# Row layout of a DRAM buffer, splits moved from GpSimd to VectorE, and token tasks of the third stage moved under the last slots of the second

## The chip, the cores and the metric

The kernel runs on one core of one Trainium2 chip. The time is the device time of one execution in microseconds; that of the kernel before is the median of three runs. Names of engines: PE is TensorE (PEld its weight loads), DVE is VectorE, ACT is ScalarE, POOL is GpSimd, SP is SyncE, which here only issues DMAs.

## The reference

Three layers follow each other on 4 x 576 = 2304 tokens of width 512.

```python
x = attention(q, k, v, s)                 # 4 batches, 8 heads of 64, causal with a bias
logits = x @ w_gate + modality_bias[modality_id]
e_idx = argmax(logits, axis=1)            # one of 8 experts per token
gate_w = softmax(logits)[range(N), e_idx]
for e in range(8):                        # first expert layer
    mask = e_idx == e
    out[mask] = gate_w[mask, None] * (relu(x[mask] @ w1[e]) @ w2[e])   # 512 -> 1024 -> 512
gate = 1.0 / (1.0 + exp(-(out @ w_gate2)))   # second layer, all tokens, 512 -> 1536
result = (gate * (out @ w_val)) @ w_out      # 1536 -> 512
```

With the inputs of this kernel two experts get 1191 and 1097 tokens, a third one 16, the others none.

## The kernel before, in words

**Attention and routing.** `Attention` works through pairs of heads, batch after batch. While it runs, `Router` keeps a queue `q` of single operations, of which one at a time is put into DVE's, PE's, POOL's and SP's program between the pieces of attention. For each of the four batches the router makes logits, the chosen expert and each token's rank in its expert. Then it writes two buffers in DRAM: `tab`, a table of 128-row scatters that POOL issues (line 669, five per batch, 128 elements of 4 bytes each: the number of a token goes to the place of its rank), and `x`, the rows of 512 values and the gate weight, 513 x 4 = 2052 bytes each (line 673, five DMAs per batch on SP).

**Slots.** `Moe` works on slots of 256 tokens of one expert: eight steps per slot, each with 12 products for the hidden layer (line 973, `ph`), and 12 for the output of the step before (line 993, `sb` or `y`). The expert's weights come as float32 (`raw`, 512 KB a DMA) and are split in a high part (ACT, line 906) and a low part, which is the difference (line 909, done by DVE for the `w1` piece and by POOL for the `w2` piece). In the first two slots (`EARLY`) these tiles are named `ew`, later `w`. `EARLY` slots begin while the router still works on the last batches; they use the expert that the first batches suggest. Beside them `main(u)` takes 14 operations of the router's queue per step (`PUMP`). At the end `slots()` (its operations are listed under line 751) computes from the counts which tokens belong to which slot: 55 small DVE operations with `row` among them, then `fetch_rows` (line 702, a POOL gather `tid<-tab`, which has to wait for all scatters into `tab`), then a transpose on PE (line 711, `itr`) and the indices `idx` with which the tokens of the later slots are gathered (line 933, `xg<-x,idx`). The transpose stands in PE's program in front of the next step's products.

**Half slots.** After the nine slots come two half slots of 128 tokens in eight half steps (lines 1077 to 1100: `hth` is a transpose on PE, `hT` its copy on DVE, `yh` the products that take it). A slot's or half slot's result is copied on ACT (`yt`, line 1005) and stored on SP (line 1007) into `x2`, the input of the third stage. A branch (line 1057, `If(more > 0)`) over additional slots follows; it isn't taken here.

**Third stage.** `Moe2` has 36 units of 42 products (line 1326: `X`, `Y`, `Z`), twelve for each third of the tokens. Before a third can start, its tokens are loaded (line 1247, four DMAs `xs<-x`) and made into seven pairs of tiles `a` by 18 tasks (`sums`): seven casts on ACT (line 1261), seven differences on DVE (line 1262) and four sums on DVE (line 1263). The tasks of the first third stand in the half slots, by `put(3, ...)` to `put(8, ...)`, which appends tasks behind a step; step 0 is the first half step. The tasks of the second and third stand in units 1 to 3.

**What sets the order.** Each engine runs its instructions in the order in which the code emits them. A task that waits keeps everything behind it on its engine waiting. The order of the work around the change is thus set by the queue `q`, by `put`, and by `spread` in `Moe2.run`, which lays a list of tasks evenly over a stretch of units.

Of the kernel before, what the change touches and what calls it, by code (L numbers as in the profile page):

```python
# [8 lines left out]
F32 = mybir.dt.float32  # L9
# [14 lines left out]
RW = 513  # L24
CAP = 2304
# [481 lines left out]
class Router:  # L507
    def __init__(self, tc, cp, ap, ps, ident, mod_bias, mod_id, x, tab, B, S):
# [28 lines left out]
        nc.gpsimd.iota(self.ids[:, :, 0:4], pattern=[[S, B], [128, 4]], base=64, **kw)  # L537
        nc.gpsimd.iota(self.ids[:, :, 4:5], pattern=[[S, B], [0, 1]], base=0, **kw)
# [18 lines left out]
    def setup_bias(self):  # L557
        nc, B, S, T = self.nc, self.B, self.S, self.T
        mb = T([128, 2, 8], "mb")
        mi = T([128, B, 5, 2], "mi", I32)  # L560
        self.space(40)
        load = lambda dst, src: self.q.append(lambda: nc.sync.dma_start(dst, src))
        load(mb, self.mod_bias.unsqueeze(0).to_broadcast([128, 2, 8]))
        m32 = self.mod_id.bitcast(I32).rearrange("(b s two) -> b s two", b=B, two=2)
        for b in range(B):
            load(mi[:, b, 0:4, :], m32[b, 64:, :].rearrange("(t p) w -> p t w", p=128))
            load(mi[:64, b, 4, :], m32[b, :64, :])
        self.space(30)
        self.q.append(lambda: self.mod_weights(mb, mi))
        nc.vector.memset(mi[64:128, :, 4, :], 0)  # L570
# [35 lines left out]
    def batch(self, b, xr, lg):  # L606
# [16 lines left out]
        q = self.q  # L623
# [42 lines left out]
        for t in range(5):  # L666
            rows, r0 = (64, 0) if t == 4 else (128, 64 + 128 * t)
            self.space(SP[b])
            q.append(lambda t=t, rows=rows: self.apart("tab", nc.gpsimd.indirect_dma_start(
                out=self.tab.rearrange("r c -> (r c)").unsqueeze(1),  # L670
                out_offset=bass.IndirectOffsetOnAxis(ap=ix[:rows, t : t + 1], axis=0),
                in_=self.ids[:rows, b, t : t + 1], in_offset=None, bounds_check=TROWS * 256 - 1, oob_is_err=True)))
            q.append(lambda t=t, rows=rows, r0=r0: nc.sync.dma_start(
                self.x[b * self.S + r0 : b * self.S + r0 + rows, :], xr[:rows, t, :]))
        if b == EARLYB - 1:
# [23 lines left out]
            q.append(self.on_guess)  # L699

# [31 lines left out]
    def slots(self):  # L732
# [76 lines left out]
        op(V.tensor_scalar, s0[0:1], s0[0:1], float(MAINH), None, ALU.is_gt)  # L809
        op(V.scalar_tensor_tensor, out=more, in0=inc[0:1, 8:9], scalar=float(MAIN), in1=s0[0:1], op0=ALU.is_gt, op1=ALU.max)  # L810
# [55 lines left out]
class Moe:  # L866
# [160 lines left out]
    def simple_slot(self, s):  # L1027
        self.gather(s)
        for k in range(4):
            self.load_slot(s, k)  # L1030
        self.gate(s)
        for h in range(2):
            self.transpose(s, h)
        for f in range(8):
            self.split(s, f)
            self.mm(s, f)
        self.finish()

    def simple_half(self, s):
        self.gather(s)  # L1040
        for k in range(4):
            self.load_slot(s, k)
        self.gate(s)
        self.half_x(s)
        for k in range(4):
            self.half(s, k)
        self.half_end()
# [7 lines left out]
    def extras(self, more):  # L1055

        with self.tc.If(more > 0):
            tt = self.r.tt
            nf = self.nc.values_load(tt[0:1, 0:1], min_val=0, max_val=SLOTS)
            nh = self.nc.values_load(tt[HROW : HROW + 1, 0:1], min_val=0, max_val=HALVES)  # L1060
            self.extra(MAIN, SLOTS, nf, self.simple_slot)
            self.extra(HROW, HROW + HALVES, nh, self.simple_half)

# [110 lines left out]
    def run(self, step):  # L1174
# [18 lines left out]
        self.hprev = None  # L1193
        step(8 * MAIN + 4 * MAINH)
        self.half_mm2(*ready)
# [6 lines left out]
class Moe2:  # L1202
# [247 lines left out]
    def load_h(self, q):  # L1450
        g, f = divmod(q, 12)
        t = self.hl[q] = self.ap.tile([128, 3, 512], F32R, tag=f"a1_{self.RING[q % 6]}", name="h0", bufs=1)[:, :, : self.G]
        self.nc.sync.dma_start(t[:, 2].bitcast(F32), self.hd[0][:, f, self.G * g : self.G * g + self.G])
# [48 lines left out]
    def p_tasks(self, j):  # L1502
# [6 lines left out]
        def high(i):  # L1509
            if i not in form:  # L1510
                form[i] = self.ap.tile([128, 2, 6, 128], F32R, tag=tags[i], name="hf", bufs=1)
            return form[i][:, 0]
# [68 lines left out]
    def rows(self):  # L1581
# [3 lines left out]
        return lambda: self.nc.vector.tensor_copy(self.row, f)  # L1585

    def run(self, ctx, rest):
# [21 lines left out]
        raws = [[], [self.ap.tile([128, 2, self.G], F32, name=f"xs{i}", bufs=1) for i in range(3)]]  # L1609
        raws[1].append(self.rp.tile([128, 1024], F32, tag="raw2_3", name="xs3", bufs=1)[:, : 2 * self.G].rearrange("p (c t) -> p c t", c=2))  # L1610
        for i in range(2):
            w = self.ap.tile([128, 2, 2, self.G], F32, tag=f"a2_{5 + i}", name="xs", bufs=1)
            raws[0] += [w[:, 0], w[:, 1]]
# [81 lines left out]
def kernel(ctx, tc, q, k, v, s, modality_id, moe_w_gate, modality_bias, w1, w2, wg, wv, wo, out):  # L1695
# [10 lines left out]
    with tc.manual_schedule():  # L1706
        ident = cp.tile([128, 128], F32, name="ident")
        make_identity(nc, ident)
        ps_ctx, at_ctx, mo_ctx, ea_ctx, mw_ctx, ex_ctx, xs_ctx, wo_ctx = (ExitStack() for _ in range(8))
        ps = pool(ps_ctx, "psum", space=PSUM)  # L1710
        rp = pool(ctx, "rawp", side="right")
        raw_tiles = lambda p, n: [(p.tile([128, 4, 256], F32, name=f"{n}1_{i}"), p.tile([128, 2, 512], F32, name=f"{n}2_{i}")) for i in range(4)]
# [17 lines left out]
        for hh in range(2):  # L1730
# [3 lines left out]
            ))  # L1734
        router.setup_bias()
# [36 lines left out]
        todo, last, xs, raws = {}, 8 * MAIN, [], []  # L1772
# [30 lines left out]
        put(2, [later])  # L1803
# [5 lines left out]
        moe.run(step)  # L1809
        xs_ctx.close()  # L1810
        ex = pool(ex_ctx, "m_extra", reuse_waits="tile")
        moe.raw, moe.pw, moe.wbufs = raw_tiles(ex, "rawx"), ex, 16
        moe.extras(more[0])
# [34 lines left out]
```

## Time and profile before

| | |
|---|---|
| median of three runs | 981.65 us (981.2 to 987.18) |
| time of the profiled execution | 984.64 us |
| its span in the profile | 982.9 us |
| mean granted TensorE clock | 0.977 |
| PE busy | 929.4 us, 95% |
| DVE, ACT, POOL busy | 710.5 us (72%), 556.6 us (57%), 410.2 us (42%) |
| moved by DMA | 124.32 MB, mean 126 GB/s |

Times in the rows below are microseconds from the start of the span. A granted clock of 1.00 is TensorE at 2.4 GHz, 0.50 at 1.2 GHz. Idle time in brackets is that of the engine just before the instruction, with what ended it.

### The profile page before, as it was taken

The page shows a single profiled execution, that of the slowest core. Times are in us where ns is not written, and L with a number is a line of the kernel's source. Part 1 is how long each engine was busy: PE and PEld are TensorE (multiplying, and loading weights), DVE is VectorE, ACT ScalarE, POOL GpSimd, SP SyncE. Part 2 cuts the span into 40 slices and gives each one's busy share as a digit, 9 for nine tenths or more (in the row PEclk, how much of TensorE's full clock was granted, in tenths as well). Part 3 has the DMA queues.
Part 4 walks back from the last instruction along what each step waited for, and adds up shares of the span by engine and source line. Part 5 has one row for each costly group of instructions (what it writes and reads, how often), then busy time and mean ns, then how long its engine had stood idle before and what let it go on. Part 6 is the DMA issues. An engine that isn't in the chain of part 4 may idle for free. (4 is left out here: it accounts for less than half of the span.)

```text
span 982.9 us, 18850 instructions
## 1 busy us (share of the span) xinstructions
PE 929.4 (95%) x6261; PEld 864.6 (88%) x6261; DVE 710.5 (72%) x1585; ACT 556.6 (57%) x1328; POOL 410.2 (42%) x627
## 2 busy tenths in 40 slices
PE   6999999999994999999999779999999999999996
PEld 5788888787784999999998769999999999889996
DVE  6889998998884668877733597576766655887771
ACT  4988888888732556655643455535444454454440
POOL 7877778888873567777640000101000000011111
PEclk8999999999997999999999889999999999999999
DMA  6654448795664145842267331232323316474411
GB/s 167 158 129 121 117 94 101 154 126 85 215 68 54 44 140 172 293 148 76 77 215 259 107 100 62 93 129 88 124 83 100 109 53 215 153 245 147 153 44 44
DMA packets 164578, 124.32 MB, mean 126 GB/s; under 512 B 86897, under 2 KB 146828, under 8 KB 164470
## 3 DMA queue, kind: packets, MB, share of 16 engines
q1 hardware_dynamic: 159462, 112.57, 43.3%
q0 software_dynamic: 3792, 10.14, 3.1%
q8 instruction: 52, 0.85, 0.4%
q14 instruction: 56, 0.46, 0.2%
q10 hardware_dynamic: 1216, 0.30, 0.2%
HBM read 115.95 MB, written 32.18 MB: 151 GB/s over the span
## 5 line engine op out<-in xcount | busy, mean ns | idle before, releaser
L1326 PE MATMUL X<-a,set 128*128 128x384 f32 x864 | 166.6, 341 | 6.5 <-ACT u L1335 3.2
L1326 PEld LDWEIGHTS X<-a,set 128*128 128x128 f32 x864 | 153.5, 191 | 9.1 <-ACT u L1335 4.0
L845 POOL TENSOR_SCALAR dn<-dr 128x256 int8<-128x256 int8 (+1 forms) x60 | 33.0, 551 | 265.2 <-DMA dr<-in_moe_w_gate_dram 121.6
L170 POOL TENSOR_SCALAR bias<-cumB,cumT 128x576 f32<-128x576 f32 (+4 forms) x155 | 82.5, 534 | 42.0 <-DVE nm L289 33.0
L909 POOL TENSOR_TENSOR w<-raw,w 128x512 fp32r<-128x512 f32 x56 | 79.3, 1427 | 42.9 <-ACT w L906 39.9
L973 PE MATMUL ph<-xT,w 128*128 128x256 f32 x672 | 91.4, 285 | 1.9 <-DVE w L909 1.9
L298 ACT ACTIVATE P<-P,nm 64x64 f32<-64x64 f32 (+4 forms) x160 | 89.7, 564 | 4.7 <-DVE nm L289 4.7
L1463 POOL DMA_INDIRECT out_dram<-oy,row x18 | 20.0, 1113 | 168.3 <-ACT oy L1487 90.6
L973 PEld LDWEIGHTS ph<-xT,w 128*128 128x128 f32 x672 | 84.9, 192 | 2.1 <-DVE w L909 2.1
L289 DVE CUSTOM_DVE_ANT_0 P<-sb,bias 128x576 f32<-128x576 f32 (+4 forms) x160 | 72.0, 479 | 17.5 <-PE sb L280 13.6
L1326 PE MATMUL Y<-a,set 128*128 128x384 f32 x432 | 81.9, 338 | 0.0
L339 DVE TENSOR_TENSOR PL<-pt,PH 128x512 fp32r<-128x512 f32 (+3 forms) x160 | 78.7, 530 | 2.4 <-ACT PH L331 1.5
L1326 PEld LDWEIGHTS Y<-a,set 128*128 128x128 f32 x432 | 76.5, 190 | 0.1
L331 ACT CAST PH<-pt 128x512 fp32r<-128x512 f32 (+3 forms) x160 | 66.6, 466 | 8.6 <-PE pt L317 6.2
L977 ACT ACTIVATE hH<-ph 128x256 fp32r<-128x256 f32 x72 | 27.7, 385 | 74.7 <-PE ph L973 74.7
L317 PE MATMUL pt<-ident,P 128*128 128x128 f32 (+2 forms) x480 | 68.5, 274 | 0.0
L909 DVE TENSOR_TENSOR w<-raw,w 128x512 fp32r<-128x512 f32 x56 | 58.9, 1053 | 12.5 <-ACT w L906 11.7
L1335 ACT COPY u<-X 128x384 f32<-128x384 f32 x72 | 34.5, 480 | 57.8 <-PE X L1326 57.7
L906 ACT CAST w<-raw 128x512 fp32r<-128x512 f32 x112 | 63.5, 619 | 0.0
L317 PEld LDWEIGHTS pt<-ident,P 128*128 128x128 f32 (+2 forms) x480 | 52.8, 130 | 10.5 <-issue 5.9
L362 PE MATMUL ot<-PH,vhl 128*128 128x512 f32 (+4 forms) x160 | 62.0, 397 | 0.0
L280 PE MATMUL sb<-KT,QH 128*128 128x288 f32 (+3 forms) x192 | 56.1, 316 | 4.9 <-DVE nm L289 4.1
(297 smaller groups left out, 2399.8 us busy)
## 6 DMA issues: line engine op xcount, KB each, us to landing
raw<-in_moe_w_dram SPq DMA_DIRECT2D x80, 512.0 KB
h<-sg SPq DMA_DIRECT2D x72, 192.0 KB
cumB<-cum_d SPq DMA_DIRECT2D x32, 288.0 KB
hp<-h SPq DMA_DIRECT2D x24, 384.0 KB
qraw<-in_q_dram SPq DMA_DIRECT2D x58, 128.0 KB
dr<-in_moe_w_out_dram SPq DMA_DIRECT2D x12, 511.6 KB
dr<-in_moe_w_gate_dram SPq DMA_DIRECT2D x24, 255.2 KB
dr<-in_moe_w_val_dram SPq DMA_DIRECT2D x24, 255.2 KB
```

Source lines behind the costliest of these rows:

```text
L170: (nc.vector if n in FILLB else nc.gpsimd).tensor_scalar(res[i][:rows], cumB[:rows, :m], -1.0, self.cumT[:rows, i, n : n + 1], ALU.mult, A ...
L280: nc.tensor.matmul(self.sb[:rows, o : o + c1 - c0], X[:, T0[i] : T0[i] + rows], h["KT"][:, c0:c1], start=j == 0, stop=j == 1)
L289: nc.vector.tensor_tensor_reduce(out=pt[:rows], in0=self.sb[:rows, o : o + m], in1=self.bias_t[n][i][:rows], op0=ALU.add, op1=ALU.min, sca ...
L298: nc.scalar.activation(h["P"][i][:rows], h["P"][i][:rows], AF.Exp, bias=h["nm", i][:rows], scale=-1.0, accum_out=self.sums_t[(n // 2) % 3] ...
L317: nc.tensor.transpose(pt[: TS[j], c : c + TS[i]], h["P"][i][: TS[i], T0[j] : T0[j] + TS[j]], self.ident[: TS[i], : TS[i]])
L331: nc.scalar.copy(t[:r, a:z], pt[:r, a:z])
L339: nc.vector.tensor_tensor(t[:r, a:z], pt[:r, a:z], h["H"][u][:r, a:z].bitcast(F32), ALU.subtract)
L362: nc.tensor.matmul(out[:, q0 : q0 + z - a], w, X[: TS[j], a:z], start=k == 0, stop=k == len(mm) - 1, skip_group_check=True)
L906: nc.scalar.copy(v, src)
L909: (eng or nc.vector).tensor_tensor(v, src, h.bitcast(F32), ALU.subtract)
L973: nc.tensor.matmul(ph, w[:, 128 * dc : 128 * dc + 128], x[:, dc], start=k == 0, stop=k == 11)
L1326: self.nc.tensor.matmul(bank, w[:, c], a[:, h, c], start=first and k == 0, stop=k == 5, skip_group_check=True)
```

## The change

It has five parts.

1. **Rows of `x` by partition.** The rows of two batches are laid out so that a partition's nine rows stand next to each other in DRAM (`XS = 9`). A batch is written with two DMAs, one of 128 pieces of 8208 bytes and one of 64 of 2052 bytes, in place of five with pieces of 2052 bytes. The token numbers in `ids` follow the new layout, and 14 small DVE operations (`Moe2.rows`, spread over units 12 to 15) turn them back for the last scatter.
2. **Low parts of the first slots on DVE.** For `EARLY` slots the low part of the `w2` piece is made by DVE as well, not by POOL.
3. **First tokens under slot 8.** The loads of the first third (`load_x(0)`) go from step 1 to step -7, their 18 tasks to steps -4 to 1, three behind each.
4. **Second tokens under the half slots.** The loads of the second third go to step 0, their tasks to steps 2 to 8 beside the weight tasks `s0`; units 1 to 3 keep only the tasks of the last third. So that the columns which these loads read hold numbers in any case, two DMAs of 512 KB fill a part of `x2` at the start, and two more tiny DVE operations in `slots()` let `more` be 1 also where the full slots hold fewer than 1536 tokens (here they hold more, so the branch is again not taken).
5. **The last half's results go out first.** Its products, the copy `yt` and the store are emitted ahead of the tasks of step 8, which end with a load of ACT's function table (`preload`).

```diff
+XS = 9
@@ Router, setup
-        nc.gpsimd.iota(self.ids[:, :, 0:4], pattern=[[S, B], [128, 4]], base=64, **kw)
-        nc.gpsimd.iota(self.ids[:, :, 4:5], pattern=[[S, B], [0, 1]], base=0, **kw)
+        kx = dict(kw, channel_multiplier=XS)
+        for a in range(2):
+            nc.gpsimd.iota(self.ids[:, 2 * a : 2 * a + 2, 0:4], pattern=[[4, 2], [1, 4]], base=2 * S * a, **kx)
...
+        for c in (1024, 1280):
+            load(self.x2.rearrange("(c p) t -> p c t", p=128)[:, :, c : c + 256], self.fill.unsqueeze(1).to_broadcast([128, 4, 256]))
@@ Router, rows of a batch
-            q.append(lambda t=t, rows=rows, r0=r0: nc.sync.dma_start(
-                self.x[b * self.S + r0 : b * self.S + r0 + rows, :], xr[:rows, t, :]))
+            if t > 2:
+                q.append(lambda t=t: self.rows_out(b, t, xr))
...
+    def rows_out(self, b, t, xr):
+        x = self.x[2 * self.S * (b // 2) : 2 * self.S * (b // 2 + 1), :].rearrange("(p j) r -> p j r", j=XS)
+        if t == 4:
+            dst, src = x[64 * (b % 2) : 64 * (b % 2) + 64, 8, :], xr[:64, 4, :]
+        else:
+            dst, src = x[:, 4 * (b % 2) : 4 * (b % 2) + 4, :], xr[:, 0:4, :]
+        self.nc.sync.dma_start(dst, src)
@@ slots
+        op(V.tensor_scalar, void[0:1], X[0:1, 3, 0:1], 4.0 * Moe2.G, None, ALU.is_lt)
+        op(V.tensor_tensor, s0[0:1], s0[0:1], void[0:1], ALU.max)
@@ Moe.split
-            self.split_piece(b[:, h, :], eng=self.nc.gpsimd, top=eng, **kw),
+            self.split_piece(b[:, h, :], eng=eng if s < EARLY else self.nc.gpsimd, top=eng, **kw),
@@ Moe.run
+        self.half_mm2(*ready)
         step(8 * MAIN + 4 * MAINH)
-        self.half_mm2(*ready)
@@ Moe2.run
-        self.room_x(1, self.ap)
-        for t in range(1, NT):
-            self.load_x(t, raws[t - 1])
-        spread(at(1, 0), at(2, 2), self.x_tasks(1, raws[0]))
-        put(at(2, 2), [lambda: self.room_x(2, self.ap)])
-        spread(at(2, 3), at(3, 4), self.x_tasks(2, raws[1]))
-        put(at(5, 0), [self.rows()])
+        self.room_x(2, self.ap)
+        self.load_x(2, raws)
+        spread(at(1, 0), at(3, 3), self.x_tasks(2, raws))
+        spread(at(12, 0), at(15, 0), self.rows())
@@ the program
-        put(1, [lambda: glu.load_x(0, raws), lambda: glu.room_x(0, keep[0])])
+        put(-7, [lambda: glu.load_x(0, raws), lambda: glu.room_x(0, keep[0])])
+        def open_second():
+            glu.second = pool(ctx, "second", reuse_waits="tile")
+            glu.room_x(1, glu.second)
+            x1.append(pool(x1_ctx, "x_second", side="right", reuse_waits="tile"))
+            raws1.extend(x1[0].tile([128, 2, glu.G], F32, name=f"xt{i}") for i in range(4))
+            glu.load_x(1, raws1)
+        put(0, [open_second])
+        def first_tokens():
+            x = glu.x_tasks(0, raws)
+            for k in range(6):
+                put(k - 4, x[3 * k : 3 * k + 3])
         def later():
-            x = glu.x_tasks(0, raws)
-            put(3, x[:4])
-            put(4, x[4:7] + s0[0])
-            put(5, s0[1] + x[7:10])
-            put(6, x[10:12] + s0[2] + s0[3])
-            put(7, s0[4] + x[12:16])
-            put(8, s0[5] + x[16:] + s0[6] + [glu.preload])
+            x, cuts = glu.x_tasks(1, raws1), (0, 3, 7, 9, 12, 15, 18, 18)
+            w = [[], [], s0[0], s0[1] + s0[2], s0[3] + s0[4], s0[5], s0[6]]
+            for k in range(7):
+                put(2 + k, w[k] + x[cuts[k] : cuts[k + 1]])
+            put(8, [glu.preload])
```

What this moves on the engines shows at three places. The first is POOL's program from the scatters of the last two batches (`tab`) to the first gather of later tokens; `ew` are the low parts of the first slots. Before:

```order
L669 DMA tab<-ids,r_ix_4655 24576x1 x5
L946 TENSOR_SCALAR xg_5158<-xg_5158 128x512 x2
L909 TENSOR_TENSOR ew<-raw_1_84,ew 128x512
L669 DMA tab<-ids,r_ix_5359 24576x1 x5
L909 TENSOR_TENSOR ew<-raw_2_86,ew 128x512 x2
L909 TENSOR_TENSOR ew<-raw_3_88,ew 128x512
L702 DMA tid<-tab,row 40x256
L909 TENSOR_TENSOR ew<-raw_3_88,ew 128x512
```

Now, from the same scatters on:

```order
L674 DMA tab<-ids,r_ix_4656 24576x1 x5
L965 TENSOR_SCALAR xg_5156<-xg_5156 128x512 x2
L674 DMA tab<-ids,r_ix_5357 24576x1 x5
L719 DMA tid<-tab,row 40x256
L1799 TENSOR_LOAD more
L952 DMA xg_5157<-x,idx 128x513 x2
```

Nothing but the scatters and the scaling of `xg` stands ahead of the gather `tid` any more.

The second is ACT at the end of the half slots; `set` are weight tasks of the third stage, `a` casts of tokens, `hh` the hidden layer of a half step, `tbl` the use of the new function table. Before:

```order
L1102 ACTIVATE hh<-phh 128x256
L1297 CAST set<-ds 128x2x256
L1261 CAST a_5_8941<-xs_7626 128x768
L1297 CAST set<-ds 128x2x256
L1261 CAST a_6_8942<-xs_7625 128x768
L1230 ACT_TABLE_LOAD
L1230 ACTIVATE tbl<-tbl 128x1
L1005 COPY yt<-yh 128x4x128
L1057 COMPARE_AND_BRANCH
```

Now:

```order
L1121 ACTIVATE hh<-phh 128x256
L1316 CAST set<-ds 128x2x256
L1280 CAST a_6_8935<-xt_8941 128x768
L1024 COPY yt<-yh 128x4x128
L1249 ACT_TABLE_LOAD
L1249 ACTIVATE tbl<-tbl 128x1
L1075 COMPARE_AND_BRANCH
```

The copy `yt` has moved ahead of the table's load, and the branch now stands behind that load.

The third is DVE in the first units of the third stage; `sg`, `p` and `u` are the units' own steps, `dd` a step on a weight. Before:

```order
L1262 TENSOR_TENSOR a_0_11971<-xs,a_0_11971 128x768
L1354 TENSOR_TENSOR p_12055<-Z,p_12055 128x384
L1356 TENSOR_TENSOR sg<-p_12055,sg 128x384
L1262 TENSOR_TENSOR a_2_11973<-xs,a_2_11973 128x768
L1263 TENSOR_TENSOR xs<-xs 128x768
L1262 TENSOR_TENSOR a_1_11972<-xs,a_1_11972 128x768
L1263 TENSOR_TENSOR xs<-xs 128x768
L1347 TENSOR_TENSOR sg<-Y,u_12020 128x384
L1263 TENSOR_TENSOR xs<-xs 128x768
```

Now:

```order
L1373 TENSOR_TENSOR p_12109<-Z,p_12109 128x384
L1375 TENSOR_TENSOR sg<-p_12109,sg 128x384
L1281 TENSOR_TENSOR a_0_12025<-xs_12021,a_0_12025 128x768
L1366 TENSOR_TENSOR sg<-Y,u_12074 128x384
L1281 TENSOR_TENSOR a_2_12027<-xs_12022,a_2_12027 128x768
L1282 TENSOR_TENSOR xs_12022<-xs_12024,xs_12022 128x768
L1373 TENSOR_TENSOR u_12165<-Y,u_12165 128x384
L1375 TENSOR_TENSOR sg<-u_12165,sg 128x384
L1281 TENSOR_TENSOR a_1_12026<-xs_12023,a_1_12026 128x768
```

Between two of the units' own steps there stand one or two of the tokens' operations where up to four stood.

## Rows read from the trace of the kernel before

**Rows 1.** Stretches of the span: length, then each engine's busy time, clock, DMA.

```profile
310.00:320.00 10.00, 6.11 (x28) 5.99 (x29) 1.48 (x4) 0.56 (x2) 6.92 (x6) 0.50 0.19 57
...
566.00:598.00 32.00, 25.43 (x117) 23.57 (x117) 28.31 (x42) 18.13 (x33) 2.15 (x4) 0.84 0.29 83
...
620.00:900.00 280.00, 279.82 (x1584) 269.75 (x1583) 190.71 (x362) 134.01 (x277) 20.25 (x38) 1.00 0.38 124
```

**Rows 2.** Waits of PE: for what, total us, times, longest.

```profile
PE itr L711 <- DMA tid<-tab,row: 9.6, 1, 9.6
...
PE ph L973 <- DVE ew L909: 4.3, 2, 2.8
...
PE X L1326 <- ACT u L1335: 3.2, 2, 2.3
PE Z L1326 <- DVE a L1262: 3.2, 1, 3.2
...
PE yh L1088 <- DVE hT L1079: 2.8, 2, 2.0
PE ph L973 <- DVE w L909: 1.9, 1, 1.9
```

**Rows 3.** Timeline of POOL at the end of routing: start, duration, instruction.

```profile
290.38 1.20 POOL L669 DMA_INDIRECT tab<-ids,r_ix  x1 [0.30 <-issue]
291.60 3.78 POOL L909 TENSOR_TENSOR ew<-raw,ew 128x512 fp32r<-128x512 f32 x3
311.05 1.03 POOL L702 DMA_INDIRECT tid<-tab,row  x1 [15.68 <-DMA tab<-ids,r_ix]
```

**Rows 4.** Scatters of line 669, third batch, then fourth: issue to landing.

```profile
DMA to landing us min/median/max: 6.9/10.1/10.9
...
DMA to landing us min/median/max: 16.0/20.2/21.4
```

**Rows 5.** DMA traffic in 284 to 293, then in 520 to 540 (weights).

```profile
DMA packets 567, 0.95 MB, mean 106 GB/s; under 512 B 103, under 2 KB 103, under 8 KB 567
...
DMA packets 5094, 6.14 MB, mean 307 GB/s; under 512 B 205, under 2 KB 4265, under 8 KB 5094
```

**Rows 6.** Timeline of PE before and after the wait for the transpose.

```profile
300.64 1.99 PE L973 MATMUL ph<-xT,ew 128*128 128x256 f32 x12
...
314.33 2.90 PE L973 MATMUL ph<-xT,ew 128*128 128x256 f32 x12 [0.26 <-PE itr L711]
```

**Rows 7.** Timeline of DVE in the first two slots.

```profile
297.15 0.69 DVE L909 TENSOR_TENSOR ew<-raw,ew 128x512 fp32r<-128x512 f32 x1
...
299.31 0.16 DVE L751 SCALAR_TENSOR_TENSOR row<-sx,s 128x1 uint32<-128x1 f32 x1
...
337.94 5.99 DVE L909 TENSOR_TENSOR w<-raw,w 128x512 fp32r<-128x512 f32 x2
```

**Rows 8.** Timeline of PE and ACT from the last half slot to the third stage.

```profile
548.86 3.66 PE L1088 MATMUL yh<-hT,raw 128*128 128x128 f32 x16 [1.97 <-DVE hT L1079]
549.35 1.28 ACT L1230 ACT_TABLE_LOAD   x1
...
552.60 0.59 ACT L1005 COPY yt<-yh 128x512 f32<-128x512 f32 x1 [1.43 <-PE yh L1088]
...
555.67 2.15 PE L1326 MATMUL X<-a,set 128*128 128x384 f32 x6 [3.15 <-ACTq L1057]
```

**Rows 9.** Timeline of PE in units 2 and 3.

```profile
589.90 3.90 PE L1326 MATMUL X<-a,set 128*128 128x384 f32 x12
...
595.72 2.24 PE L1326 MATMUL X<-a,set 128*128 128x384 f32 x12
```

**Rows 10.** DVE's groups of instructions in 566 to 598: busy us, mean ns.

```profile
L1262 DVE TENSOR_TENSOR a<-xs,a 128x768 fp32r<-128x768 f32 x14 | 13.4, 954 | 4.0 <-ACT a L1261 3.5
L1263 DVE TENSOR_TENSOR xs<-xs,xs 128x768 f32<-128x768 f32 x4 | 4.0, 1006 | 0.0
L1263 DVE TENSOR_TENSOR xs<-xs 128x768 f32<-128x768 f32 x4 | 3.8, 950 | 0.0
```

More of the change, by code (lines that the diff above doesn't have):

```diff
@@ L666, in batch @@
         for t in range(5):
-            rows, r0 = (64, 0) if t == 4 else (128, 64 + 128 * t)
+            rows = 64 if t == 4 else 128
             self.space(SP[b])
@@ L1028, in simple_slot @@
         self.gather(s)
-        for k in range(4):
-            self.load_slot(s, k)
         self.gate(s)
@@ L1034, in simple_slot @@
         for f in range(8):
+            if f % 2 == 0:
+                self.load_slot(s, f // 2)
             self.split(s, f)
@@ L1040, in simple_half @@
         self.gather(s)
-        for k in range(4):
-            self.load_slot(s, k)
         self.gate(s)
@@ L1053, in extra, with extras @@
                 self.extra(s + 1, end, n, do)
-    def extras(self, more):
+    def extras(self, more, again):
         with self.tc.If(more > 0):
@@ L1062, in extras @@
             self.extra(HROW, HROW + HALVES, nh, self.simple_half)
+            again()
     def half_x(self, s):
@@ L1510, in high @@
             if i not in form:
-                form[i] = self.ap.tile([128, 2, 6, 128], F32R, tag=tags[i], name="hf", bufs=1)
+                form[i] = (self.second if tags[i][0] == "a" else self.ap).tile([128, 2, 6, 128], F32R, tag=tags[i], name="hf", bufs=1)
             return form[i][:, 0]
@@ L1584, in rows @@
         self.nc.sync.dma_start(f, self.ids2[0, :2304].rearrange("(t p) -> p t", p=128))
-        return lambda: self.nc.vector.tensor_copy(self.row, f)
+        V, a, p, j, c = self.nc.vector, *(self.keep.tile([128, 18], F32, name=f"row{n}") for n in "apjc")
+        n = float(2 * self.r.S)
+        return [lambda f=f, args=args, kw=kw: f(*args, **kw) for f, args, kw in (
+            (V.tensor_scalar, (a, f, n, n, ALU.is_ge, ALU.mult), {}),
+            (V.tensor_tensor, (j, f, a, ALU.subtract), {}),
+            (V.tensor_scalar, (p, j, -4.0, 1.0 / XS, ALU.add, ALU.mult), {}),
+            (V.tensor_scalar, (p, p, 12582912.0, None, ALU.add), {}),
+            (V.tensor_scalar, (p, p, -12582912.0, None, ALU.add), {}),
+            (V.scalar_tensor_tensor, (), dict(out=j, in0=p, scalar=-float(XS), in1=j, op0=ALU.mult, op1=ALU.add)),
+            (V.tensor_tensor, (a, a, p, ALU.add), {}),
+            (V.scalar_tensor_tensor, (), dict(out=a, in0=j, scalar=128.0, in1=a, op0=ALU.mult, op1=ALU.add)),
+            (V.tensor_scalar, (c, j, 4.0, 64.0, ALU.is_ge, ALU.mult), {}),
+            (V.scalar_tensor_tensor, (), dict(out=a, in0=c, scalar=64.0, in1=a, op0=ALU.add, op1=ALU.add)),
+            (V.tensor_scalar, (p, p, 64.0, 512.0, ALU.is_ge, ALU.mult), {}),
+            (V.tensor_scalar, (p, p, -n, None, ALU.add), {}),
+            (V.scalar_tensor_tensor, (), dict(out=p, in0=j, scalar=8.0, in1=p, op0=ALU.is_equal, op1=ALU.mult)),
+            (V.tensor_tensor, (self.row, a, p, ALU.add), {}),
+        )]
     def run(self, ctx, rest):
@@ L1708 @@
         make_identity(nc, ident)
-        ps_ctx, at_ctx, mo_ctx, ea_ctx, mw_ctx, ex_ctx, xs_ctx, wo_ctx = (ExitStack() for _ in range(8))
+        ps_ctx, at_ctx, mo_ctx, ea_ctx, mw_ctx, ex_ctx, xs_ctx, wo_ctx, x1_ctx = (ExitStack() for _ in range(9))
         ps = pool(ps_ctx, "psum", space=PSUM)
         rp = pool(ctx, "rawp", side="right")
-        raw_tiles = lambda p, n: [(p.tile([128, 4, 256], F32, name=f"{n}1_{i}"), p.tile([128, 2, 512], F32, name=f"{n}2_{i}")) for i in range(4)]
+        raw_tiles = lambda p, n, k=4: [(p.tile([128, 4, 256], F32, name=f"{n}1_{i}"), p.tile([128, 2, 512], F32, name=f"{n}2_{i}")) for i in range(k)]
         raw = raw_tiles(rp, "raw")
@@ L1734 @@
             ))
+        router.x2 = x2
         router.setup_bias()
@@ L1771 @@
         glu = Moe2(tc, moe, x2, ids2, wg, wv, wo, out, hd, keep[0], rp, wo32)
-        todo, last, xs, raws = {}, 8 * MAIN, [], []
+        todo, last, xs, raws, x1, raws1 = {}, 8 * MAIN, [], [], [], []
         def put(at, tasks):
@@ L1809, with again @@
         moe.run(step)
+        x1_ctx.close()
         xs_ctx.close()
         ex = pool(ex_ctx, "m_extra", reuse_waits="tile")
-        moe.raw, moe.pw, moe.wbufs = raw_tiles(ex, "rawx"), ex, 16
-        moe.extras(more[0])
+        moe.raw, moe.pw, moe.wbufs = 2 * raw_tiles(ex, "rawx", 2), ex, 8
+        def again():
+            at = [ex.tile([128, 1024], F32, tag=f"rawx{1 + i // 2}_{i % 2}", name="xa", bufs=1)[:, : 2 * glu.G] for i in range(4)]
+            at = [a.rearrange("p (c t) -> p c t", c=2) for a in at]
+            glu.load_x(1, at)
+            for task in glu.x_tasks(1, at):
+                task()
+        moe.extras(more[0], again)
         ex_ctx.close()
```

14 lines of the change are left out of this document (7 added, 7 removed).

## The prediction

> **What bounds the kernel now.** I read the waits of PE first, since PE is busy 95% of the span, then the stretches around those waits, then the timelines of the engines that PE waited for. In the third stage PE works without a pause: 279.82 of 280 us between 620 and 900, 1584 products, so 0.177 us each at full clock [rows 1]. Most of what can be won lies in four places where PE waits.
>
> The largest is one wait of 9.6 us for the transpose `itr` at the end of routing [rows 2]. The chain runs backwards from PE over the POOL gather `tid`, which starts at 311.05 after 15.68 us of idle time, to the last scatter into `tab`, issued at 290.38 [rows 3]. The scatters of the third batch land 6.9 to 10.9 us after their issue, those of the fourth 16.0 to 21.4 [rows 4]. In that stretch the DMA engines move 106 GB/s, nearly all of it rows of `x`, where weights move at 307 [rows 5]. The other input of the gather, `row`, is ready on DVE at 299.31 [rows 7], so the landing comes last, by more than 11 us. After the wait PE is at the lower of its clocks (granted 0.50 from 310 to 320 [rows 1]): twelve products take 2.90 us that took 1.99 before [rows 6].
>
> The second is the stretch 566 to 598: 117 products, which at 0.177 are 20.7 us of work, in 32 us. So 11.3 us are lost there, 6.4 of them as waits for ACT's copies `u` and DVE's tokens `a` [rows 2], the rest mostly by the lower clock (3.90 us for a group that later takes 2.24 [rows 9]). DVE is busy for 28.31 of the 32 us [rows 1], 21.2 of them with the tokens of two thirds [rows 10]. DVE is the bound there.
>
> The other two are small: 1.9 us for a low part `w`, after two of DVE's splits took 5.99 us together [rows 2, 7], and the way from the last half slot to the third stage, where the products `yh` wait 1.97 us for `hT` and the first product `X` waits 3.15 [rows 8].
>
> **The change part by part.** *Rows of x, and the gather.* Between the scatters of the third and fourth batch one split of 1.26 us (a third of 3.78 [rows 3]) leaves POOL. So I put the last scatter's issue at 289.1 and not 290.38. What its landing then takes the trace doesn't show. The lower bound is 6.9 us, the upper one 20.2 [rows 4]. I take 10.9, the slowest of the third batch: those scatters too had rows of `x` beside them, but less of a backlog, and the change leaves a fourth of the pieces. That is a landing at 300.0. DVE's `row` then matters as well: three more splits of 0.69 stand ahead of it, which would make 301.4, but DVE no longer runs beside POOL's splits there, so that I leave it at about 300. From `tid` to the next products PE took 314.33 - 311.05 = 3.28 us [rows 3, 6]. So PE goes on at 303.3 in place of 314.33: -11.0. In 310 to 320 PE was busy for 6.11 us at half clock, of which 3.05 are lost; with a wait of 3 us or none I count half of that as won, -1.5. Together -12.5. The bounds: the late landing (309.3) leaves about -2, the early one -15, as the two waits of 4.3 us for `ew` [rows 2], now hidden ahead of the long wait, would then count as well.
>
> *Low parts on DVE.* In both first slots DVE gets another split of 0.69 us per step [rows 7] for thirteen steps, 9 us in all. In the steps without router work DVE has room for it. In those with fourteen router operations DVE becomes the slowest engine, but what it delays there ends in the wait for `tid`, which is in the term above. If that cover goes, it costs up to three splits, 2 us. What goes is POOL's split ahead of the main slots' first ones, where DVE's two splits stretched to 5.99 us and PE waited 1.9. POOL's three splits of the next slot stay beside them, so I count -1.5, from 0 to -2.8 (1.9, and 0.9 for one group at half clock [rows 6]).
>
> *Tokens of the second third out of units 1 to 3.* Of DVE's 28.3 us in 566 to 598, half of 21.2 goes. The remaining 17.7 are less than the 20.7 that the products need, and less than two tokens' operations as a rule stand between the units' own steps. I count -10.0 of the 11.3; the rest is left for operations that still stand ahead of `sg`. The bounds are -11.3, and -5 if DVE's order and not its sum made half of the loss.
>
> *The same tasks under slot 8 and the half slots.* Before, 18 tasks stood in six half steps, and PE lost 2.8 us there in two waits for `hT` behind them [rows 2]. Now 36 tasks stand in thirteen steps, three or four in most. They wait for more loads: those of the second third stand on SP behind a store and ahead of the second half slot's weights, 4 x 393 KB, 5.1 us at 307 GB/s [rows 5], the same place nearly as the first third's before. A cast that waits on ACT holds back the hidden layer behind it. The tasks in slot 8 run while POOL splits only in the first two of the steps. I count +1.0, from 0 to +4 (two more waits like the longest).
>
> *Last half first.* `yt` is free of the table's load, but the load of 1.28 us, until now under the products `yh`, comes between `yt` and the branch for which `X` waits; `yt` ended at 553.19, `X` began 2.48 us later [rows 8]. DVE's copy `hT` still stands behind two token operations. So I count +1.0, from -1.5 (`hT` on time, the load hidden) to +2.
>
> *The rest.* The fill of 1 MB lies under attention; 14 small operations on DVE lie under units in which PE is the bound [rows 1], 2.2 us if nothing covered them at 0.16 each [rows 7]; the two in `slots()` come behind `row`. Nothing, at most +1.
>
> The sum is -12.5 - 1.5 - 10.0 + 1.0 + 1.0 = -22.0. The profiled execution took 984.64 us, 3.0 above the median of the three runs, so it would take 962.6; against the median of 981.65 the forecast is 959.6.
>
> **The rivals.** *The scatters wait for bytes, not for pieces.* The rows hold as many bytes as before, 2.3 MB for two batches. If these go out at 106 GB/s [rows 5] however they are cut, the last scatter lands at about 309 again and the first term is -2: 981.65 - 11.5 = 970.1. For it: weights in pieces that are no longer move at 307 GB/s, so the size of the pieces alone is not what makes 106. Against it: the third batch's scatters, with the same bytes ahead, landed twice as fast. The Trainium skill, in "DMA: Bandwidth & Descriptors", section "Specifications", puts full rate at 512 bytes and more; by that, 2052 bytes were long enough, and the time would be this rival's. The rows agree as far as weights go. The same page, section "Queues, rings and completion order", says that an engine changes from one queue to another only after a whole packet of descriptors; by that, longer pieces let a scatter wait longer, not less. No row shows it.
>
> *Units 1 to 3 stay DVE's.* If the eleven operations left, with the units' own, still come late by their order, 5 of the 10 us come back: 964.6. Against it speaks the sum of 17.7 in 20.7 us; for it that DVE waits for ACT's casts there too [rows 10].
>
> *The slots pay.* The token operations stand ahead of `hL` or `hT` in twelve steps. One such wait took 1.97 us, and the sixteen products behind it 3.66 [rows 8], at half clock, so 1.83 more: 3.8 a step. If nine of the twelve lose that, it is 34 us against the 23 that the other terms give: 992.7, slower than before. It decides from 1.9 us a step in all twelve. Against it: before, with the same number of tasks per step, two steps of six lost 2.8 us together.
>
> **How the numbers follow.** I give the forecast 0.62, the bytes 0.20, the units 0.13, the slots 0.05. The range goes from all terms at their lower bounds, -15 - 2.8 - 11.3 - 1.5 = -30.6, or 951, to the first rival's 970, and leaves out its upper half, the slots and a part of mixtures of the two rivals that win less. A difference of 1% (9.8 us) is about what a measurement of this kernel tells from none: faster means under 971.8. The forecast, the units and two thirds of the bytes lie below, 0.88; 0.08 is within 1%, for the bytes with a cost in the slots; 0.04 is slower.
>
> **What the profile after would show.** The first term is right if the fourth batch's scatters land within 11 us and `tid` starts near 300; it is wrong if their median stays at 16 or more. Units 1 to 3 are right if PE has no wait over 1 us for `a` or `u` and a granted clock near 1.00 there; wrong if DVE is still busy nine tenths. The costs show as waits for `hT`, `hL` or `hh` in slot 8 and the half slots, and as the time from `yt` to `X`, which I expect at 3.5 to 4 us. The whole would be wrong if a new wait for the rows of `x` (`xg`) or for SP's loads stood where the old ones were.

## The result and the profile after

The changed kernel took 958.78 us (median of four runs, 955.08 to 961.6) against 981.42 of the kernel before beside it: a ratio of 0.976, interval 0.9732 to 0.9788. Run again later (`f1_after` below) it took 963.32 against 982.27, 0.9796, from 0.9772 to 0.982. The forecast was 959.6.

Both traces hold the same 6261 products on PE in nearly the same order, so the n-th product of one can be set beside the n-th of the other. This table gives the start of some of them, and what a stretch between two gave (the profiled executions took 984.64 and 959.78 us).

| up to the product that before starts at | start after | lead | gained in the stretch | forecast |
|---|---|---|---|---|
| 282.11 (attention) | 280.35 | 1.76 | 1.8 | 0 |
| 321.11 (routing, `itr`) | 310.51 | 10.61 | 8.8 | 12.5 |
| 350.11 (first main slot) | 335.79 | 14.33 | 3.7 | 1.5 |
| 504.10 (slots) | 488.68 | 15.42 | 1.1 | 0 |
| 546.06 (slot 8, half slots) | 531.84 | 14.22 | -1.2 | -1.0 |
| 566.23 (end of the half slots, unit 1) | 548.95 | 17.28 | 3.1 | -1.0 |
| 598.15 (units 2, 3) | 571.05 | 27.09 | 9.8 | 10.0 |
| 900.11 (later units) | 876.41 | 23.70 | -3.4 | 0 |
| 974.65 (last product) | 950.14 | 24.51 | 0.8 | 0 |

The sum is close, the terms less so. The first row can't be put down to the change: in the profiles of the kernels below, the same product starts between 277.9 and 289.6, so the end of attention varies by more than the 1.8 us gained here. The waits of PE in the kernel after, to be read beside [rows 2] (total, times, longest):

```profile
PE yh L1107 <- DVE hT L1098: 3.0, 3, 1.3
PE X L1345 <- ACTq L1075: 2.8, 1, 2.8
PE ph L992 <- DVE ew L928: 2.8, 3, 1.8
...
PE ph L992 <- DVE rg L768: 1.1, 1, 1.1
PE itr L728 <- DMA tid<-tab,row: 1.0, 1, 1.0
...
PE X L1345 <- ACT u L1354: 0.8, 2, 0.5
```

The wait for `itr` has fallen from 9.6 us to 1.0. Those for `u` are down from 3.2 to 0.8, those for `a` and `w` are gone from the list's head, and `hT` is as before. The timeline of POOL at the end of routing answers to [rows 3] (first scatter of the third batch, last two of the fourth, gather):

```profile
274.30 1.10 POOL L674 DMA_INDIRECT tab<-ids,r_ix  x1 [5.61 <-DVE r_ix L667]
...
287.35 0.97 POOL L674 DMA_INDIRECT tab<-ids,r_ix  x1 [0.30 <-issue]
291.69 0.92 POOL L674 DMA_INDIRECT tab<-ids,r_ix  x1 [3.36 <-DMA tab<-ids,r_ix]
300.85 1.03 POOL L719 DMA_INDIRECT tid<-tab,row  x1 [8.24 <-DVE el L768]
```

The gather starts at 300.85, where 300.0 was forecast, but on another way. The last scatter isn't issued at 289.1: it first waits 3.36 us for an older scatter to land, and the gather follows some 9 us behind its issue. (The releaser `el` is named because it came last by the profile; the gather's other input, `row`, starts on DVE at 297.72.) The rows of `x` aren't through when it is issued: the last packet of theirs ends at 296.70, where it ended at 309.80 before. PE then goes on at 304.87, because DVE, busy with two splits in each step with router work, brings `rg` 1.1 us late:

```profile
303.42 0.32 PE L728 MATMUL itr<-ident,tid 40*128 40x40 f32 x2 [0.96 <-DMA tid<-tab,row]
304.87 1.99 PE L992 MATMUL ph<-xT,ew 128*128 128x256 f32 x12 [1.13 <-DVE rg L768]
```

In units 2 and 3 the stretch of 120 products now takes 23 us and not 32 for 117 [rows 1], at a granted clock of 1.00; DVE is busy for 19.48 of them, 0.85 of the stretch. In the later units, though, 80 us hold 457 products where they held 462 (windows after, after, before: length, then busy time and count of PE, PEld, DVE, ACT, POOL, then clock, DMA share and GB/s):

```profile
548.00:571.00 23.00, 21.89 (x120) 20.63 (x120) 19.48 (x33) 13.89 (x28) 1.98 (x4) 1.00 0.26 80
...
680.00:760.00 80.00, 80.00 (x457) 80.00 (x456) 52.08 (x113) 38.01 (x85) 5.76 (x14) 1.00 0.28 92
...
680.00:760.00 80.00, 80.00 (x462) 79.94 (x461) 55.23 (x119) 37.38 (x83) 5.87 (x14) 1.00 0.33 106
```

The way from the half slots to the third stage answers to [rows 8]:

```profile
533.77 2.05 PE L1107 MATMUL yh<-hT,raw 128*128 128x128 f32 x16 [1.10 <-DVE hT L1098]
...
535.90 0.59 ACT L1024 COPY yt<-yh 128x512 f32<-128x512 f32 x1 [3.51 <-issue]
536.51 1.28 ACT L1249 ACT_TABLE_LOAD   x1
...
538.66 2.29 PE L1345 MATMUL X<-a,set 128*128 128x384 f32 x6 [2.84 <-ACTq L1075]
```

`X` starts 2.2 us after the end of `yt` (2.48 before, 3.5 to 4 expected). The branch doesn't wait until the table's load has ended at 537.79: its record on ACT stands at 535.97, before the load begins. And `yh` takes 2.05 us at a granted clock of 1.00, where it took 3.66 at 0.53.

### The profile page after: what moved, and what is told of

Its sections match the earlier page's. It is cut to its first block, busy times and chain, and to the rows that moved or that the text cites. A ratio compares the mean times of both kernels' runs of the same rounds, so it can differ in the third digit from the quotient of the medians.

```text
span 958.0 us, 18838 instructions
## 1 busy us (share of the span) xinstructions
PE 923.8 (96%) x6261; PEld 859.8 (90%) x6261; DVE 708.4 (74%) x1613; ACT 556.7 (58%) x1328; POOL 395.9 (41%) x616
## 5 line engine op out<-in xcount | busy, mean ns | idle before, releaser
L290 DVE CUSTOM_DVE_ANT_0 P<-sb,bias 128x576 f32<-128x576 f32 (+4 forms) x160 | 72.1, 480 | 19.4 <-PE sb L281 16.5
L928 DVE TENSOR_TENSOR w<-raw,w 128x512 fp32r<-128x512 f32 x56 | 55.4, 989 | 10.2 <-ACT w L925 9.4
```

The costliest lines, as they stand in the source:

```text
L290: nc.vector.tensor_tensor_reduce(out=pt[:rows], in0=self.sb[:rows, o : o + m], in1=self.bias_t[n][i][:rows], op0=ALU.add, op1=ALU.min, sca ...
L928: (eng or nc.vector).tensor_tensor(v, src, h.bitcast(F32), ALU.subtract)
```

## The experiments

Twelve runs followed, in three groups; each group shares its runs of the kernel before (median 987.72 in the first, 982.11 in the second, 982.27 in the third). What a part gives is worked out from its ratio; the difference of the two medians comes out a little otherwise. The measure that turned out to tell most about the routing is the time from the third batch's first scatter to the gather `tid`: 35.2 us before (275.88 to 311.05), 26.6 in the first profile after (274.30 to 300.85).

**One part alone, and one part less.** `e1_rows` is the kernel before with part 1 alone:

```diff
+            if t > 2:
+                q.append(lambda t=t: self.rows_out(b, t, xr))
-            q.append(lambda t=t, rows=rows, r0=r0: nc.sync.dma_start(
-                self.x[b * self.S + r0 : b * self.S + r0 + rows, :], xr[:rows, t, :]))
```

> Only the rows of x are laid out by partition and written in pieces of 8208 bytes; splits and tokens as before. If the many pieces held up the scatters, the wait for itr falls from 9.6 us to under 4, all of the fourth batch's scatters have landed near 300 to 303 on the scale of the kernel before (310 there), and the time is 8 to 11 us less, about 972. If the bytes hold them up, they land at 307 or later, the wait stays above 7 us, and the time is 979 to 981.

Measured: 982.14 us against 987.72, ratio 0.9921 (0.9897 to 0.9946), 7.8 us less by the ratio (the medians are 5.6 apart). The wait for `itr` is 1.0 us. The gather starts 30.5 us after the first scatter, in the timeline of POOL:

```profile
276.86 1.09 POOL L672 DMA_INDIRECT tab<-ids,r_ix  x1 [5.64 <-DVE r_ix L665]
...
296.67 0.91 POOL L672 DMA_INDIRECT tab<-ids,r_ix  x1 [4.53 <-issue]
307.36 1.03 POOL L717 DMA_INDIRECT tid<-tab,row  x1 [6.02 <-DVE sz L766]
```

The layout does what was forecast, though 5 and not 11 us sooner, and the gain is just under the 8 us expected at the least. The short wait for `itr` says less than it seems: the last scatter waits 4.53 us, POOL's splits stand behind it, and PE now waits 4.3 us for one of them ahead of the gather.

```profile
298.93 0.80 PE L1008 MATMUL sb<-hH,ew 128*128 128x256 f32 x2 [4.33 <-POOL ew L924]
```

So the stretch of routing gains only 4.6 us here (product at 282.11 before to the one at 321.11), against 8.8 in the kernel after, where part 2 has taken the splits off POOL. In `e2_splits`, part 2 alone, it loses 1.7.

`e2_splits` is the kernel before with part 2 alone.

```diff
-            self.split_piece(b[:, h, :], eng=self.nc.gpsimd, top=eng, **kw),
+            self.split_piece(b[:, h, :], eng=eng if s < EARLY else self.nc.gpsimd, top=eng, **kw),
```

> Only the low parts of the first slots go from POOL to DVE. If POOL's split ahead of the main slots' first ones was the reason of the stretched DVE splits there, the wait of 1.9 us for w and the lower clock after it go, 3 to 4 us; the wait for itr stays at 8 us or more, because the rows still hold up the scatters: about 977.5. If DVE becomes the bound of the first slots instead, the wait for ew grows and the time is 981 to 984.

Measured: 981.44, ratio 0.9941 (0.9909 to 0.9972), 5.8 us less by the ratio (medians 6.3). The first main slot is without a pause, and the two splits that took 5.99 us [rows 7] take 2.38 (window, then DVE's timeline):

```profile
337.00:350.00 13.00, 13.00 (x112) 13.00 (x111) 9.18 (x15) 9.34 (x20) 5.96 (x4) 1.00 0.25 73
```

```profile
341.45 2.38 DVE L909 TENSOR_TENSOR w<-raw,w 128x512 fp32r<-128x512 f32 x2
```

The gather still starts 38 us after the first scatter (277.23 to 315.19), and PE waits 6.3 us for it. So the splits didn't hold back the gather; they cost in the slot behind it. The stretch of the first main slot gains 3.7 us, more than the forecast's bound; 1.5 of these also come in `e1_rows`, `e3_tokens` and `e6_wide`, which split as before, as the granted clock stays at 1.00 there behind the same wait (0.87 in the kernel before, from 337 to 350).

`e3_tokens` is the kernel before with parts 3 to 5 alone, `e4_no_rows` the kernel after without part 1.

> Only the tokens' tasks move (first third under slot 8, second under the half slots, last half's results first); rows and splits as before. Units 1 to 3 give 10 us, the way to the third stage 3, the half slots cost 1: about 969. The third stage's later units ran 1.3% slower in the kernel after (175 against 173 ns a product, 3 us). If that comes from where the tiles of the second third lie, it shows here too, and not in the two runs before; if from the chip, it shows anywhere. If units 1 to 3 give only half, 974.

Measured: 979.23, ratio 0.9891 (0.9836 to 0.9946), 10.8 us less by the ratio (medians 8.5). From the product at 566.23 before to the one at 598.15, the lead grows by 9.8 us, exactly as in the kernel after; slot 8 and the half slots cost 1.9. DVE is no longer the bound (window of units 2 and 3):

```profile
569.00:592.00 23.00, 21.78 (x123) 20.82 (x122) 19.20 (x32) 13.44 (x28) 1.92 (x3) 1.00 0.26 81
```

The later units run as fast as before, so where the second third's tiles lie isn't what slows them.

> The kernel after with the rows of x laid out and written as before. If the pieces are the reason, the wait for itr is back at 8 us or more, at the lower clock behind it, and the time is 966 to 969. If POOL's splits (which are gone here) were what held back the gather, the wait stays under 3 us and the time is 959 to 961.

Measured: 972.96 us, ratio 0.9841 (0.9781 to 0.99); 0.9841 of 981.42 is 965.8, at the edge of what the first theory gave. The gather starts 35.0 us after the first scatter (280.09 to 315.12), as before. The expected long wait for `itr` isn't there: PE waits 3.6 us for it, and 6.5 us a few steps earlier for a hidden layer behind ACT. So the length of one wait is a poor measure, the time of the gather a good one. The three parts alone add up to 7.8 + 5.8 + 10.8 = 24.4 us, against 23.6 for the whole by its ratio (by medians 20.4 against 22.7).

**Pieces, bytes, boundaries.** `e5_pieces` keeps the new layout and writes it in rows of 2052 bytes:

```diff
-            if t > 2:
-                q.append(lambda t=t: self.rows_out(b, t, xr))
+            q.append(lambda t=t: self.rows_out(b, t, xr))
-            dst, src = x[:, 4 * (b % 2) : 4 * (b % 2) + 4, :], xr[:, 0:4, :]
+            dst, src = x[:, 4 * (b % 2) + t, :], xr[:, t, :]
```

> The kernel after, with its layout of x, but each partition's rows written one by one: four DMAs of 128 pieces of 2052 bytes per batch in place of one of 8208. If the size of the pieces is what counts, the scatters land late as with the rows as before, and the ratio to the kernel before is that of the run without the new layout, 0.984. If the layout or the bytes count, it stays at 0.976.

Measured: 966.71 against 982.11, ratio 0.9825 (0.9766 to 0.9883). The interval takes in both expectations; the trace decides. The wait for `itr` is 9.6 us, the gather starts 31.6 us after the first scatter:

```profile
281.38 1.10 POOL L674 DMA_INDIRECT tab<-ids,r_ix  x1 [7.20 <-DVE r_ix L667]
...
296.33 0.91 POOL L674 DMA_INDIRECT tab<-ids,r_ix  x1 [1.31 <-DMA tab<-ids,r_ix]
312.96 1.03 POOL L718 DMA_INDIRECT tid<-tab,row  x1 [15.71 <-DMA tab<-ids,r_ix]
```

So about half of the gain in the gather's start comes with the two large writes per batch (31.6 to the 28 or so of the unchanged kernel, below) and about half is there without them (35.0 to 31.6). This rests on one trace, of the slowest of the four executions (971.88 us). In the time until the last packet of rows is through, counted from the first scatter, the large writes make most of it: 32.9 us in `e4_no_rows`, 31.0 here, 21.6 to 26.5 in the profiles with large pieces, where the gather then starts 3.3 to 5.6 us later (here 0.6). The size of the pieces wasn't separated from the number of DMAs per batch (two in place of five) and the moment of their issue, and what of the layout makes the rest wasn't tried.

`e6_wide` is the kernel before with `RW = 576`, and zeros in the added columns.

> The kernel before with rows of x of 576 values, 2304 bytes, a multiple of 256, in place of 2052; the 63 values behind the gate weight are zeros and aren't used. If pieces that begin and end off such a boundary make the writes slow, the writes drain sooner although there are 12% more bytes, the wait for itr falls below 7 us and the time by 3 us or more. If bytes or the number of pieces make it, the wait is as long or a microsecond longer and the time the same or 1 us more.

Measured: 980.2 against 982.11, ratio 0.9976 (0.9946 to 1.0005). The wait for `itr` is 7.0 us and the gather starts 33.6 us after the first scatter (276.30 to 309.87), so at most a small part lies in the boundaries.

`f1_after` is the kernel after once more, `f4_twice` writes each row a second time:

```diff
         self.nc.sync.dma_start(dst, src)
+        self.nc.sync.dma_start(dst2, src)
```

> The kernel after, unchanged, on the same chip as the three below. In other executions the gather tid started 29 to 31 us after the third batch's first scatter, 26.6 in the one profiled first, 35 to 38 with the rows as before. If 26.6 was a lucky one, this one shows about 29, a wait for itr of 5 us or more, and a ratio of 0.977.

Measured: 963.32 against 982.27, ratio 0.9796 (0.9772 to 0.982). The profile shows what was expected: 28.4 us from the first scatter to the gather, and a wait of 6.0 us. It also has the landings of the fourth batch's scatters, which the first profile lacks (all but the last one's): a median of 17.0 us behind their issue, where the prediction named up to 11 as right and 16 or more as wrong.

```profile
275.57 1.10 POOL L674 DMA_INDIRECT tab<-ids,r_ix  x1 [5.02 <-DVE r_ix L667]
...
287.65 0.97 POOL L674 DMA_INDIRECT tab<-ids,r_ix  x1 [0.30 <-issue]
294.20 0.96 POOL L674 DMA_INDIRECT tab<-ids,r_ix  x1 [5.58 <-DMA tab<-ids,r_ix]
304.00 1.03 POOL L719 DMA_INDIRECT tid<-tab,row  x1 [8.84 <-DMA tab<-ids,r_ix]
```

```profile
PE itr L728 <- DMA tid<-tab,row: 6.0, 1, 6.0
```

```profile
DMA to landing us min/median/max: 15.2/17.0/18.4
```

> The kernel after with every row written a second time into a DRAM buffer that nobody reads: twice the bytes and twice the pieces of 8208 bytes, the same scatters. If the gather waits for all writes to drain, tid starts 8 to 10 us later and the time is 7 to 10 us more than that of the unchanged one. If it waits for the scatters' own time, it is within 2 us.

Measured: 971.84, ratio 0.9883 (0.9858 to 0.9908), 8.5 us more than the unchanged kernel beside it. The gather starts 36.6 us after the first scatter, 8.2 later, and PE waits 14.8 us:

```profile
278.02 1.10 POOL L674 DMA_INDIRECT tab<-ids,r_ix  x1 [4.98 <-DVE r_ix L667]
...
314.63 1.04 POOL L723 DMA_INDIRECT tid<-tab,row  x1 [17.56 <-DMA tab<-ids,r_ix]
```

```profile
PE itr L732 <- DMA tid<-tab,row: 14.8, 1, 14.8
```

The last packet of rows ends at 314.82, in `f1_after` at 299.62. So the scatters land, and the gather starts, only when the writes are all but through, and bytes count: 2.4 MB more are 8.2 us. The first rival of the prediction was right about bytes, and wrong in that the way in which they are cut and laid out counts too.

**The last half first.** `e8_last` is the kernel after with part 5 undone.

```diff
-        self.half_mm2(*ready)
         step(8 * MAIN + 4 * MAINH)
+        self.half_mm2(*ready)
```

> The kernel after with the last half slot's products, copy and store behind the tasks of step 8 again. By the step of the prediction that costed this part at +1.0, it is 1 us faster than the kernel after, ratio 0.975. By what the profile after shows (the branch didn't wait for the table's load), it is the same or up to 1 us slower, 0.976 to 0.977.

Measured: 962.57 against 982.11, ratio 0.9798 (0.9741 to 0.9855), too wide to tell a microsecond. In the trace the way from the start of `yh` to `X` takes 4.9 us, as in the kernel after: `X` starts 2.1 us after the end of `yt` (537.24 + 0.59), with the table's load far ahead of both.

```profile
533.75 1.28 ACT L1249 ACT_TABLE_LOAD   x1
...
537.24 0.59 ACT L1024 COPY yt<-yh 128x512 f32<-128x512 f32 x1 [1.34 <-PE yh L1107]
...
539.97 1.31 PE L1345 MATMUL X<-a,set 128*128 128x384 f32 x6 [2.81 <-ACTq L1075]
```

Part 5 shows no gain and no cost in these traces. The 3.1 us of that stretch came from elsewhere: in `e1_rows`, which has none of parts 3 to 5, `yh` waits 1.96 us for `hT` as before and yet runs at full clock, and that stretch is 1.9 us shorter than before too; in `e2_splits`, likewise without them, it is 3.6 us shorter.

```profile
542.68 2.05 PE L1103 MATMUL yh<-hT,raw 128*128 128x128 f32 x16 [1.96 <-DVE hT L1094]
```

**The slower third stage.** The later units were slow in the kernel after and in `e1_rows`, and not in `e2_splits`, `e3_tokens` and `e4_no_rows`. Part 1 separates the two, and of it only the fourteen operations and their four tiles lie in the third stage. `e9_pad`, and again `f2_pad` beside the unchanged kernel, make the tiles wider:

```diff
-*(self.keep.tile([128, 18], F32, name=f"row{n}") for n in "apjc")
+*(self.keep.tile([128, 32], F32, name=f"row{n}")[:, :18] for n in "apjc")
```

> The kernel after with the four small tiles of the row numbers 128 bytes per partition wide in place of 72, so that what lies behind them in SBUF moves by 512 bytes against the kernel before and not by 288. The third stage ran at 175 ns a product in the two runs with these tiles and at 173 in the four without. If the place of the tiles behind them is the reason, the pitch is 173 again and the time 3 us less than that of the kernel after: ratio 0.973. If the fourteen operations themselves are, it stays at 175 and 0.976.

Measured for `e9_pad`: 962.55 against 982.11, ratio 0.9789 (0.9735 to 0.9844), but a pitch of 173 ns in the third stage.

> The kernel after with the row numbers' tiles padded to 128 bytes, against the unchanged one beside it: 3 us less, ratio 0.974, with 173 ns a product in the third stage against 175. If other things move it as much, the two are equal.

Measured: 960.82, ratio 0.9778 (0.9756 to 0.9801), against 963.32 and 0.9796 of the unchanged kernel. The medians differ by 2.5 us; the intervals overlap, so the time alone doesn't prove it. The windows of the third stage do, 462 products in 80 us against 456 (`f2_pad`, then `f1_after`):

```profile
680.00:760.00 80.00, 80.00 (x462) 79.94 (x462) 53.13 (x114) 38.31 (x86) 5.86 (x14) 1.00 0.30 96
```

```profile
680.00:760.00 80.00, 80.00 (x456) 80.00 (x456) 51.61 (x111) 38.44 (x86) 5.98 (x14) 1.00 0.29 94
```

The commonest distance between two products is 173 ns against 175, and all fourteen traces agree: 175 in the six with the tiles as they were written, 173 in the three with padding and in the five without the tiles. The fourteen operations are the same in both, so it is the place in SBUF of what lies behind the tiles. The later units (from the product at 598.15 before to the one at 900.11) take 301.8 us with the padding and 305.2 without it in this group. But the place counts in the slots too, the other way round: from the product at 350.11 to the one at 504.10 the slots take 154.2 us with the padding and 152.9 without. So padding wins some 2 us and not 3, and the slots' gain of 1.1 us in the table, which nobody forecast, comes with the same tiles.

`f3_pad_wide` adds rows of 576 values.

> As the padded one, with rows of x of 576 values: pieces of 9216 bytes, all at multiples of 256. If pieces off that boundary cost time, tid starts 2 to 3 us sooner after the first scatter and the time is 1 to 3 us less than with padding alone. If bytes cost, 12% more of them put it 1 us later.

Measured: 960.76, ratio 0.9784 (0.976 to 0.9808), the same as with padding alone; the gather starts 29.4 us after the first scatter. The boundaries don't show here either. The two padded kernels have the lowest medians of their group.

## Why the prediction was right

The total was right to a microsecond, the range held, and the two largest mechanisms were the ones named. That the total is so close is luck in part: the first term came out 3.7 us short in the first profile and the later units lost 3.4, while the small terms came out 6 us better and attention and the slots gave 2.9 that weren't forecast. Run again, the median was 963.32. Point by point:

- **Rows of x, and the gather: -12.5, measured -8.8 in the first profile** and -7.3 in the one of `f1_after`; -5.4 in `e9_pad`, which has the same rows and splits. This is the term that was mis-sized. The step that failed is the scatter: I let it go at 289.1 and land after 10.9 us. It waits for an older one to land, so it is issued 17.4 to 19.2 us after the first scatter, where I had 13.2, and the gather follows 9 to 11 us later. By the sign that I had set, the landing is wrong: the scatters of the fourth batch still land 15.2 to 18.4 us after their issue in `f1_after`. The third batch's, from which I took 10.9, land later than before too, up to 16.5 us after their issue in `f3_pad_wide` and 16.3 in `f4_twice`. The rows are through sooner, and with them the scatters. That the gather began at 300.85, near 300.0, is chance: attention ended 1.8 us earlier in that execution. From the first scatter 24.1 us were forecast, and 26.6 to 29.8 measured. Of the clock's loss I had counted half as won, 1.5 us. The two steps behind the transpose took 8.46 us before, 7.32 after and 7.75 in `f1_after`, so 1.1 and 0.7 were won; the late `rg` took 0.7 back.
- **Low parts on DVE: -1.5, measured -3.7,** beyond the bound of 2.8. `e2_splits` shows all of it: the wait of 1.9 us and the lower clock after it both go. I had counted one group at half clock behind the wait, and there were two. With the splits as before, the three kernels named above still gain 1.5 there, as the clock stays up behind the same wait of 1.9. What part 2 itself gives is therefore 2.2 us where the clock stays up, and 3.7 against an execution in which it fell. That it also keeps the splits from standing behind the last scatter I had not counted (`e1_rows`).
- **Units 1 to 3: -10.0, measured -9.8,** also in `e3_tokens`. DVE's sum against PE's was the right measure, and the rival that gave half of it back fell: the longest wait for `u` is 0.5 us, and the granted clock 1.00.
- **Slot 8 and the half slots: +1.0, measured +1.2,** as three waits for `hT` of 1.3 us and less. The slow rival needed 1.9 us in each of twelve steps.
- **Last half first: +1.0, measured -3.1,** the wrong sign. The step that failed is the table's load "between `yt` and the branch": the branch doesn't wait for it. The gain is a shorter wait for `hT` (1.10 for 1.97, in `e8_last` without the part too) and a clock that stayed up, which it did in kernels without the part as well. It belongs to the execution in which the kernel before was profiled, more than to part 5.
- **The rest: 0, measured +3.4 in the later units and -1.1 in the slots.** The fourteen operations were hidden, as I said; that their tiles move others in SBUF I didn't see. This cost happens to stand against the small terms that came out better.

The bytes' rival had 0.20, and by it some 2 us of the first term were left. `e1_rows` gives 7.8 us in all, and in `e5_pieces` pieces of 2052 bytes in place of 8208 lose part of the gain; here small scatters stand beside the writes. The rule of the Trainium skill that stood for this rival ("DMA: Bandwidth & Descriptors", section "Specifications": full rate from 512 bytes) therefore doesn't settle this case.

## What to carry to other kernels

A gather that depends on scatters may wait for all writes ahead of them, so the price of a buffer's rows is read from the last landing, not from the scatters' own time; here few and long pieces were through 6 us sooner at the least, and twice the bytes put the gather off by 8.2 us. A scatter that waits for an older one holds up what stands behind it on its engine, so move that work first. An engine whose sum of work exceeds PE's in a stretch is worth relieving until its sum lies below PE's; what then comes back is the time that PE lost there, and that forecast held to 0.2 us. When a change adds small tiles to a pool, look at the pitch of the products in every stage: 288 bytes cost some 3 us in one stage and gave some 1 us in another. A sum of terms that meets the total is no proof of the terms.

## What the runs showed of the hardware

- The pitch of the third stage's products is 173 or 175 ns, depending on whether the tiles behind four small ones are moved by 512 or by 288 bytes per partition, at the same granted clock of 1.00. In the slots the smaller move is the faster one, 152.9 us against 154.2 (`f1_after`, `f2_pad`). Why isn't known from these runs.
- A scatter of 128 elements of 4 bytes took 6.9 us from issue to landing at the least in the kernel before [rows 4], 15.2 to 18.4 us behind the rows in `f1_after`, and 20.5 to 22.5 behind twice the rows in `f4_twice`. From the last one's issue to the gather that waits for it, 9 to 11 us passed in the kernels with long pieces, while the rows still drained.
- After the same wait of 1.96 us for `hT` the granted clock fell in one execution (0.53, `yh` 3.66 us [rows 8]) and not in another (1.00 and 2.05 us, `e1_rows`). A term of 2 us that hangs on this can't be forecast from one profile.
